# Attention and two feed-forward layers on one core: the softmax row sums of two head pairs in one PSUM bank, in 12 passes where there were 16

## The chip, the cores and the metric

The kernel runs on one core of a Trainium2 chip. The metric is device time in microseconds (us): the median over several executions. One more execution is recorded by the hardware profiler; the rows below come from it. PE is TensorE's matmul side, PEld its weight loads, DVE is VectorE, ACT ScalarE, POOL GpSimd, and SP issues DMAs.

## The reference

Batch 2, 12 heads, 448 positions, head width 64. Softcapped attention, then a gated layer behind an RMS norm, then a second layer with a leaky activation:

```python
scores = cap * np.tanh(scale * np.matmul(q, k.transpose(0, 1, 3, 2)) / cap)
attn = np.exp(scores - np.max(scores, axis=-1, keepdims=True))
attn = attn / (np.sum(attn, axis=-1, keepdims=True) + 1e-09)
x = np.matmul(attn, v)                     # then heads are put side by side: 896 x 768
rms = np.sqrt(np.mean(x * x, axis=-1, keepdims=True) + 1e-06)
xn = x / rms * rms_g
g = xn @ w_gate
x = (g * sigmoid(g) * (xn @ w_val)) @ w_out
h = x @ w_in
out = (np.maximum(h, 0) + alpha * np.minimum(h, 0)) @ w_out2
```

All of it is in fp32. This study is about the sum over a row of `attn` and what is done with its reciprocal.

## The kernel before, in words

The 24 heads are worked on as 12 **pairs**, numbered 0 to 11; two pairs that follow each other (0 and 1, 2 and 3, ...) form a **group**, numbered 0 to 5, and the program keeps them in `group` and `members`. One pass of the loop over `i` computes the scores of pair `i` and finishes pair `i - 1`. The order of the work is written out by hand: each engine has one queue of instructions that it takes in order, and a step that waits holds up everything behind it on its engine.

In iteration `i` TensorE does, in this order: for even `i` from 4 on, two *spread* matmuls of the pairs `i - 4` and `i - 3` (in `norm`, on `sel_t` and `r2`, before and after the first piece of scores); the scores of pair `i` in four pieces (`qk`); the row sums of pair `i - 1` (`sums`); the product of the weights with v of pair `i - 1` (`pv`, into `oo`). ScalarE takes the scores through tanh and exp (`soft`) into `pt`, seven tiles of 128 x 448 a pair: three keys' blocks of each of the two heads, and a seventh with the last 64 keys of both heads.

The row sums become a factor on the output on a way through several engines:

1. `sums(i)` sums over the 128 keys of a tile with a matmul whose weights are ones, 32 columns wide, so that four such matmuls run side by side in four column groups. Eight of them (the seventh tile counts twice, with half of the ones zeroed, `half`) fill four strips of 32 equal rows in the bank `us[i]`, two strips a head.
2. `evac_u(i)` copies the bank to `us` in SBUF (DVE) and issues two DMAs that lay the 448 sums of a row on 16 partitions (`gt`).
3. `recip(n)`, in the odd iteration after the group's second pair, adds the two strips and epsilon (`gf`), takes the reciprocal, splits it into a rounded part `th` and a rest `tl` (all DVE, 64 x 28 elements), and issues two DMAs that put both into `r2`.
4. The spread matmuls read `r2` in the next even iteration, and DVE multiplies the kept output `ee` by what they give (`xf`).

DVE also copies `oo` to `ee` (`evac_o`), splits q and k of the next pair into two parts `hi` and `lo` (`prep`), and unpacks the weights for the layers behind the attention (`w_bits`, into `wt`; `w_top`, `w_hi`, `w_lo`). POOL squares `xf` for the RMS norm (`square`) and adds weight tiles (`w_sum`, in `wt`). Which of these small steps stand in which iteration is set by two tables, `first` (filled by `a`) and `second` (filled by `z`), ahead of the loop. `xf`, `wt`, `th` and the other names are those of the rows below.

Of the kernel before, what the change touches and what calls it, by code (L numbers as in the profile page):

```python
# [35 lines left out]
Q = 32  # L36
K3 = KD // 2
# [20 lines left out]
def attn_moe_kernel(ctx: ExitStack, tc: tile.TileContext, units, qk_in, v, sel, w, gvec, alpha, out):  # L58
# [22 lines left out]
    half = aconst.tile([P, 2, D], F32, name="half")  # L81
# [116 lines left out]
    def third():  # L198
        return ps_x.tile([P, 2, 512], F32, tag="x", name="s")
# [41 lines left out]
    def tiles_of(i):  # L241
        return [pt[i][:, min(n, TILES - 1)] for n in range(TILES + 1)]
# [23 lines left out]
    def evac_u(i, queues=(nc.sync, nc.sync)):  # L266

        n, j = group[i]
        if j == 0:
            gt[n] = sb.tile([4 * RP, 2, S // RP], F32, tag="gt", name="gt")  # L270
        u = sb.tile([P, S], F32, tag="us", name="us")
        nc.vector.tensor_copy(u, us.pop(i)[:, :S])
        r0 = 2 * RP * j
        for k, q in enumerate(queues):
            q.dma_start(
                out=gt[n][r0:r0 + 2 * RP, k, :], in_=u[k * Q:P:D].rearrange("h (p s) -> h p s", p=RP)
            )

    def recip(n, queues=(nc.sync, nc.sync)):
        t = gt.pop(n)  # L280
        w = 2 * len(members[n])
        m = slice(0, w * RP)
        f = sb.tile([4 * RP, S // RP], F32, tag="gf", name="gf")
        nc.vector.scalar_tensor_tensor(
            out=f[m], in0=t[m, 0], scalar=eps_t[m], in1=t[m, 1], op0=ALU.add, op1=ALU.add
        )
        nc.vector.reciprocal(out=f[m], in_=f[m])
        th = sb.tile([4 * RP, S // RP], F32R, tag="th", name="th")
        tl = sb.tile([4 * RP, S // RP], F32R, tag="tl", name="tl")
        nc.vector.tensor_copy(th[m], f[m])  # L290
        nc.vector.tensor_tensor(out=tl[m], in0=f[m], in1=th[m], op=ALU.subtract)
        rr = r2[n % 2]
        for r0, x, q in zip((0, 32), (th, tl), queues):
            row = rr[r0:r0 + w].rearrange("r (p s) -> r p s", p=RP)
            q.dma_start(out=row.bitcast(F32), in_=x[m].bitcast(F32))
# [20 lines left out]
    def under():  # L316
        return ps_r.tile([P, 512], F32, tag="u", name="rps")

    def norm(i, rps):
        b, p = divmod(i, NP)  # L320
        n, j = group[i]
        nc.tensor.matmul(rps[:, :S], sel_t[:, j, :], r2[n % 2], start=True, stop=True)
        nc.vector.tensor_tensor(out=xf[b][:, p, :], in0=ee.pop(i), in1=rps[:, :S], op=ALU.mult)

# [89 lines left out]
    with tc.manual_schedule():  # L414
# [6 lines left out]
        nc.vector.memset(half, 0.0)  # L421
        for h in range(2):
            nc.vector.memset(half[h * D:h * D + D, h], 1.0)
# [37 lines left out]
        def a(i, fn, *args):  # L461
            first.setdefault(i, []).append((fn, args))
# [13 lines left out]
        for i in range(NPAIR):  # L476
            a(i, load_raw, i + 2)
# [29 lines left out]
        for i in range(NPAIR):  # L507
# [35 lines left out]
            if i:  # L543
                evac_u(i - 1)
                if i > 1:
                    pv(i - 1)
                del pt[i - 1], hi[i - 1], lo[i - 1], vt[i - 1]
# [4 lines left out]
        norm(last - 3, third()[:, 0])  # L552
        norm(last - 2, under())
# [3 lines left out]
        evac_u(last, (nc.sync, nc.scalar))  # L557
# [3 lines left out]
        def pair_tile(pool, tag):  # L561
            return pool.tile([P, 2, 512], F32, tag=tag, name=tag)

# [17 lines left out]
        product(pb[1], ("g", 1, "A12"), "B21", True, rows=(0,), span=range(6))  # L581
# [7 lines left out]
        product(pb[1], ("g", 1, "A12"), "B21", True, rows=(0,), span=range(6, 3 * K3))  # L589
# [13 lines left out]
        n_chain = [0]  # L603

        def chain_pair():
            n_chain[0] += 1
            return pair_tile(*((ps_x, "x") if n_chain[0] % 2 else (pm, "m")))

# [58 lines left out]
        for g in range(2):  # L667
            keep_part(d11, g, pb, lambda: h_of(g)[:, 2:])
            pa[g] = chain_pair()
            product(pa[g], ("g", g, "A11"), "B11", True, cuts={} if g else {(0, 4): SHORT})  # L670
# [675 lines left out]
```

## Time and profile before

| | |
|---|---|
| median of 3 runs | 552.42 us (552.24 to 552.92) |
| the profiled execution, time | 552.85 us |
| the profiled execution, span from first to last instruction | 551.1 us |
| mean granted clock of TensorE, as a share of full speed | 0.999 |
| busy: PE, PEld | 545.6 us (99%), 461.3 us (84%) |
| busy: DVE, ACT, POOL | 448.5 us (81%), 370.6 us (67%), 98.8 us (18%) |
| attention, up to the first product of the layers | 100.6 us of the span |

A row of the timeline reads: start in us from the start of the span, length in us, engine (a q behind it means its sequencer, which issues), line, operation, what is written<-what is read, shape, and how many alike are merged; in brackets the idle time of the engine just before it and what ended that. Instructions of one engine overlap by up to a tenth of a microsecond at their ends, and matmuls more. An fp32 matmul is two PE instructions, so eight matmuls are 16 instructions in a row's count.

### The profile page before, as it was taken

What the parts mean: (1) busy time and instruction counts of PE and PEld (TensorE: products, weight loads), DVE (VectorE), ACT (ScalarE), POOL (GpSimd) and SP (SyncE); (2) the same over time, 40 slices, a digit from 0 to 9 for tenths busy, and PEclk for the clock granted to TensorE, in tenths of its full rate; (3) what the DMA queues carried; (4) which work ended last, traced back from release to release, by engine and by line L of the source; (5) the groups of instructions that cost most, each with busy time, mean ns of one, the idle gap of its engine ahead of it and who ended that gap; (6) DMA issues with size and microseconds to landing.
All of it is one profiled execution on the core that took longest, in us unless ns stands there. A gap on an engine that the chain in (4) does not pass through costs nothing.

```text
span 551.1 us, 7691 instructions
## 1 busy us (share of the span) xinstructions
PE 545.6 (99%) x3061; PEld 461.3 (84%) x3061; DVE 448.5 (81%) x511; ACT 370.6 (67%) x433; POOL 98.8 (18%) x54
## 2 busy tenths in 40 slices
PE   8999999999999999999999999999999999999997
PEld 5444544699999999999999999999999999999996
DVE  4698889898999967878889898979866899999242
ACT  7989999477766554576757554787967996467110
POOL 0034663300065231010000048101111000000000
PEclk9999999999999999999999999999999999999999
DMA  7756420400334534065510573005512267013022
GB/s 253 260 188 197 164 73 8 163 12 1 120 120 162 178 110 171 1 228 173 184 46 1 229 230 114 1 0 173 172 58 69 105 203 255 0 59 115 0 101 100
DMA packets 17316, 66.09 MB, mean 120 GB/s; under 512 B 3584, under 2 KB 5504, under 8 KB 17280
## 3 DMA queue, kind: packets, MB, share of 16 engines
q1 hardware_dynamic: 16746, 65.08, 34.9%
q8 instruction: 24, 0.39, 0.3%
q10 hardware_dynamic: 390, 0.39, 0.2%
q0 software_dynamic: 144, 0.13, 0.1%
q14 instruction: 12, 0.10, 0.1%
HBM read 62.66 MB, written 2.75 MB: 119 GB/s over the span
## 4 chain that ended last, share of the span: by engine, by line
PE 96%; DVE 1%; ACT 1%; DMA 1%; issue 0%; DVEq 0%
PE s L395 19%; PE x L395 13%; PE m L395 13%; PE s L775 9%; PE s L749 8%; PE x L775 7%; PE oo L236 6%; PE s L207 5%; PE x L749 4%; PE m L775 4%; PE rps L249 3%; PE m L749 2%; PE s L408 1%; PE m L408 1%; PE x L408 1%; ACT pt L221 1%
## 5 line engine op out<-in xcount | busy, mean ns | idle before, releaser
L133 ACT CAST wh<-wt 128x768 fp32r<-128x768 f32 x105 | 87.1, 832 | 66.4 <-PE s L775 24.9
L139 DVE TENSOR_TENSOR wl<-wt,wh 128x768 fp32r<-128x768 f32 x108 | 113.6, 1053 | 12.5 <-ACT wh L133 12.2
L126 POOL TENSOR_TENSOR wt<-wt 128x768 f32<-128x768 f32 x33 | 75.1, 2284 | 265.9 <-DVE wt L118 97.9
L113 ACT CAST top<-raw 128x768 f16<-128x768 bf16 x64 | 68.8, 1076 | 27.0 <-DMA raw<-w_in 11.7
L118 DVE SCALAR_TENSOR_TENSOR wt<-raw,top 128x768 uint32<-128x768 uint32 x68 | 69.8, 1028 | 1.5 <-ACT top L113 1.5
L395 PE MATMUL s<-xx,wh 128*128 128x448 f32 x264 | 63.5, 364 | 0.0
L395 PEld LDWEIGHTS s<-xx,wh 128*128 128x128 f32 x264 | 49.4, 187 | 4.6 <-issue 0.7
L395 PE MATMUL x<-xx,wh 128*128 128x448 f32 x204 | 49.9, 366 | 0.0
L395 PE MATMUL m<-xx,wh 128*128 128x448 f32 x204 | 49.5, 364 | 0.0
L619 DVE TENSOR_TENSOR xx<-b,xx 128x896 fp32r<-128x896 f32 (+1 forms) x40 | 48.8, 1228 | 0.6 <-ACT xx L632 0.6
L216 ACT ACTIVATE pt<-s,cinv 128x896 f32<-128x896 f32 (+1 forms) x48 | 41.1, 911 | 6.2 <-PE s L207 5.9
L395 PEld LDWEIGHTS x<-xx,wh 128*128 128x128 f32 x204 | 38.2, 188 | 3.5 <-issue 0.4
L395 PEld LDWEIGHTS m<-xx,wh 128*128 128x128 f32 x204 | 38.2, 187 | 3.0
L775 PE MATMUL s<-xx,wh 128*128 128x448 f32 x132 | 40.0, 362 | 0.0
L236 PE MATMUL oo<-pt,vt 128*32 128x448 f32 x384 | 38.5, 540 | 0.4 <-ACT pt L221 0.3
L221 ACT ACTIVATE pt<-pt,cap_t 128x3136 f32<-128x3136 f32 (+2 forms) x13 | 35.3, 2714 | 0.4
L395 PE MATMUL s<-xx,wl 128*128 128x448 f32 x132 | 33.8, 364 | 0.0
L236 PEld LDWEIGHTS oo<-pt,vt 128*32 128x32 f32 x384 | 12.2, 110 | 23.6 <-issue 21.4
L775 PE MATMUL x<-xx,wh 128*128 128x448 f32 x104 | 31.2, 362 | 0.0
L749 PE MATMUL s<-xx,wh 128*128 128x448 f32 x96 | 27.2, 364 | 0.0
L775 PEld LDWEIGHTS s<-xx,wh 128*128 128x128 f32 x132 | 24.7, 187 | 2.1
L775 PE MATMUL s<-xx,wl 128*128 128x448 f32 x72 | 26.5, 367 | 0.0
(223 smaller groups left out, 1119.0 us busy)
## 6 DMA issues: line engine op xcount, KB each, us to landing
raw<-w_in SPq DMA_DIRECT2D x68, 768.0 KB
rw<-qk_in SPq DMA_DIRECT2D x11, 480.0 KB
vt<-v_in SPq DMA_DIRECT2D x12, 256.0 KB
out<-b SPq DMA_DIRECT2D x2, 448.0 KB
out<-b SPq DMA_DIRECT2D x2, 224.0 KB
out<-e SPq DMA_DIRECT2D x1, 448.0 KB
out<-c SPq DMA_DIRECT2D x2, 224.0 KB
gt<-us SPq DMA_DIRECT2D x23, 3.5 KB
```

Of the source, the lines that this page charges most:

```text
L113: copy(top_of[u].bitcast(F16)[:, 1::2], raw_t[u].bitcast(BF16)[:, 4:4 * n + 4:4])
L118: nc.vector.scalar_tensor_tensor(out=f_t[u].bitcast(U32), in0=raw_t.pop(u).bitcast(U32)[:, 1:2 * n + 1:2], scalar=13, in1=top_of.pop(u), o ...
L126: add(out=t, in0=f_t[a], in1=f_t[b], op=op)
L133: copy(h_t[u], f_t[u].rearrange("p (k m) -> p k m", m=P))
L139: nc.vector.tensor_tensor(out=l_t[u], in0=f_t[u].rearrange("p (k m) -> p k m", m=P), in1=h_t[u], op=ALU.subtract)
L216: nc.scalar.activation(out=t[:, 2 * g:2 * g + w], in_=st.pop((i, g))[:, :w, :S], func=AF.Tanh, scale=cinv)
L221: nc.scalar.activation(out=t[:, done:to], in_=t[:, done:to], func=AF.Exp, scale=cap_t)
L236: nc.tensor.matmul(oo[i][q * Q:q * Q + Q, :S], vv[:, n, q % 2 * Q:q % 2 * Q + Q], t[:, min(n, TILES - 1), :], start=c == 0, stop=c == TG, ...
L395: nc.tensor.matmul(ps[:, r, c0:c1], lhs, rhs[:, c0:c1], start=first and n == 0, stop=n == len(mm) - 1, skip_group_check=True,)
L619: nc.vector.tensor_tensor(out=out, in0=a, in1=b, op=op)
L749: nc.tensor.matmul(dst[m], wt[:, kk * MB + m, :], x, start=first and u == 0 and kk == 0 and n == 0, stop=u == 1 and kk == 1 and n == 2, sk ...
L775: nc.tensor.matmul(dst[m], wt[:, kk * MB + m, :], x, start=start and ks + kk == 0 and i == 0, stop=fin and last and kk == 1 and i == 2, sk ...
```

## The change

- A group's two pairs share one PSUM bank (`row_sum[n]`). Its four strips of 32 rows now hold four different rows each, picked by where ones stand in the weights: `strip` is a 56-column strip of zeros with 8 columns of ones, and a window of 32 columns of it puts a tile's sums on one of four groups of 8 rows. The seventh tile of a pair goes through once, with its own strip of half ones.
- For the group's first pair DVE adds the first two tiles to the next two (`add_halves`, 128 x 896, into `tp`), and TensorE sums the result in place of the four. With this the first pair has 4 matmuls in its own turn, and the second pair's turn has 8: one that is left of the first pair and its own seven. That makes 12 a group; before it was 8 and 8.
- `evac_u` runs once a group, with one copy and four DMAs of 64 partitions in place of two copies and two DMAs each. `recip` starts with one more DVE add, over 64 x 56 elements.
- The first spread matmul of a group writes to the second bank of the score tile that follows it, in place of the row-sum bank, and its multiplication by `ee` (`scaled`) stands behind it.
- Two casts and splits of weights for the layers (`w_hi`, `w_lo` of the first two of `conv`) stand one iteration later.
- Behind the loop, three matmuls of the layers stand ahead of the last two spreads that stood behind them, and three more ahead of the RMS sum.

The core of the diff:

```diff
+    def add_halves(i):
+        t = half_sum[i] = sb.tile([P, 2, S], F32, tag="tp", name="tp", bufs=1)
+        nc.vector.tensor_tensor(out=t, in0=pt[i][:, 0:2], in1=pt[i][:, 2:4], op=ALU.add)
 
     def sums(i):
-        us[i] = ps_s.tile([P, 2, 512], F32, tag="s", name="us")[:, 0] if i == NPAIR - 1 else under()
-        for n, t in enumerate(tiles_of(i)):
-            q = n % 2 * D + n // 2 % 2 * Q
+        n, j = group[i]
+        t, at_ = pt[i], lambda h: (0, 3 * UNIT - (2 * j + h) * UNIT)
+        tail = (t[:, TILES - 1], (1, 3 * UNIT - 2 * j * UNIT))
+        whole = [(t[:, c], at_(c % 2)) for c in range(TILES - 1)]
+        if j == 0:
+            row_sum[n] = under()
+            x = half_sum[i]
+            half_sum[i] = [(x[:, h], at_(h)) for h in range(2)]
+            steps = [*whole[4:], tail, half_sum[i][0]]
+        else:
+            steps = [half_sum.pop(i - 1)[1], *whole, tail]
+        for q, (x, (k, c)) in enumerate(steps):
+            q0 = q % 4 * Q
             nc.tensor.matmul(
-                us[i][q:q + Q, :S], half[:, n % 2, :Q] if n > 5 else ones[:, :Q], t, start=n < 4, stop=n > 3,
+                row_sum[n][q0:q0 + Q, :S], strip[:, k, c:c + Q], x, start=j == 0, stop=j == 1 and q > 3,
                 skip_group_check=True,
             )
...
+    def evac_u(n, queues=4 * (nc.sync,)):
+        gt[n] = sb.tile([4 * RP, 4, S // RP], F32, tag="gt", name="gt", bufs=1)
+        u = sb.tile([P, S], F32, tag="us", name="us", bufs=1)
+        nc.vector.tensor_copy(u, row_sum.pop(n)[:, :S])
+        for k in range(4):
+            queues[k].dma_start(
+                out=gt[n][:, k, :], in_=u[k * Q:k * Q + Q:UNIT].rearrange("r (p s) -> r p s", p=RP)
+            )
...
     def recip(n, queues=(nc.sync, nc.sync)):
         t = gt.pop(n)
+        nc.vector.tensor_tensor(out=t[:, 0:2], in0=t[:, 0:2], in1=t[:, 2:4], op=ALU.add)
...
         for i in range(NPAIR):
+            if i % 2 == 0:
+                (a if i else z)(i and i + 1, add_halves, i)
             a(i, load_raw, i + 2)
...
-        for n, j in ((3, 0), (4, 1), (9, 6)):
+        for n, j in ((4, 0), (5, 1), (9, 6)):
             z(n, w_hi, conv[j], nc.vector.tensor_copy)
...
-            if pairs:
-                norm(i - 4, under())
             if i:
                 home = {1: (ps_r, "u"), 2: (ps_o, "o")}.get(i)
-                qk(i, TG, home[0].tile([P, 1, 512], F32, tag=home[1], name="s") if home else third())
+                t = home[0].tile([P, 1, 512], F32, tag=home[1], name="s") if home else third()
+                if pairs:
+                    spread(i - 4, t[:, 1])
+                qk(i, TG, t)
+                if pairs:
+                    scaled(i - 4, t[:, 1])
...
-        product(pb[1], ("g", 1, "A12"), "B21", True, rows=(0,), span=range(6))
+        product(pb[1], ("g", 1, "A12"), "B21", True, rows=(0,))
         norm(last - 1, under())
...
+        pa[0] = chain_pair()
+        product(pa[0], ("g", 0, "A11"), "B11", True, rows=(0,), span=range(3))
         rms_sum(B - 1, upper("ms"))
```

What the change does to the queues is seen in two places. The first is DVE's queue in an odd iteration of the loop (iteration 7), from the copy of pair 5's output on; before it reads:

```order
L264 COPY ee<-oo 128x448
L190 CAST hi<-rw 128x960
L191 TENSOR_TENSOR lo<-rw,hi 128x960
L284 SCALAR_TENSOR_TENSOR gf<-gt,eps_t 64x28
L287 RECIPROCAL gf<-gf 64x28
L290 CAST th<-gf 64x28
L291 TENSOR_TENSOR tl<-gf,th 64x28
L118 SCALAR_TENSOR_TENSOR wt<-raw,top_95 128x768
L272 COPY us<-rps 128x448
```

After the change the same place of DVE's queue reads:

```order
L278 COPY ee<-oo 128x448
L246 TENSOR_TENSOR tp<-pt 128x896
L191 CAST hi<-rw 128x960
L192 TENSOR_TENSOR lo<-rw,hi 128x960
L292 TENSOR_TENSOR gt<-gt 64x56
L296 SCALAR_TENSOR_TENSOR gf<-gt,eps_t 64x28
L299 RECIPROCAL gf<-gf 64x28
L300 CAST th<-gf 64x28
L301 TENSOR_TENSOR tl<-gf,th 64x28
L119 SCALAR_TENSOR_TENSOR wt<-raw,top_95 128x768
```

The two new adds, `tp` and `gt`, stand ahead of the reciprocal, and the copy `us` of an even pair, which stood behind it, is gone.

The second place is TensorE's queue where iteration 7 ends and iteration 8 begins (the row sums of pair 6, the product with v, the first spread of group 2, and the first scores of pair 8); before it reads:

```order
L249 MATMUL rps<-pt,ones 32x448 x6
L249 MATMUL rps<-pt,half 32x448 x2
L236 MATMUL oo<-pt,vt 32x448 x16
L322 MATMUL rps<-r_0_92,sel_t 128x448
L207 MATMUL s<-hi 128x448
```

After the change it reads:

```order
L263 MATMUL rps<-pt,strip 32x448 x3
L263 MATMUL rps<-tp,strip 32x448
L237 MATMUL oo<-pt,vt 32x448 x16
L330 MATMUL s<-r_0_92,sel_t 128x448
L208 MATMUL s<-hi 128x448
```

Four of the eight matmuls are gone, the last that is left reads DVE's sum `tp`, and the spread that reads `r2` stands ahead of the scores as it did.

## Rows read from the trace of the kernel before

**Rows 1.** The page, busy time in us, share of the span, instructions.

```profile
PE 545.6 (99%) x3061; PEld 461.3 (84%) x3061; DVE 448.5 (81%) x511; ACT 370.6 (67%) x433; POOL 98.8 (18%) x54
```

**Rows 2.** Timeline of PE: pair 7's row sums, then its product with v.

```profile
66.09 1.32 PE L249 MATMUL rps<-pt,ones 128*32 128x448 f32 x10
...
67.62 3.19 PE L236 MATMUL oo<-pt,vt 128*32 128x448 f32 x32
```

**Rows 3.** Timeline of PE: the first spread matmul of groups 0 to 3.

```profile
32.11 0.47 PE L322 MATMUL rps<-r,sel_t 128*128 128x448 f32 x1
...
47.48 0.47 PE L322 MATMUL rps<-r,sel_t 128*128 128x448 f32 x1
...
62.86 0.47 PE L322 MATMUL rps<-r,sel_t 128*128 128x448 f32 x1
...
79.51 0.47 PE L322 MATMUL rps<-r,sel_t 128*128 128x448 f32 x1 [0.19 <-DVE us L272]
```

**Rows 4.** Timeline of SP: the DMAs of `tl`, and of `gt`.

```profile
29.42 0.57 SPq L295 DMA_DIRECT2D r<-tl  x1
...
39.13 1.09 SPq L275 DMA_DIRECT2D gt<-us  x2
...
60.48 0.58 SPq L295 DMA_DIRECT2D r<-tl  x1
```

**Rows 5.** Timelines of ACT and PE: the exps of pairs 1 and 2, pair 1's sums.

```profile
16.66 2.92 ACT L221 ACTIVATE pt<-pt,cap_t 128x3136 f32<-128x3136 f32 x1
...
22.82 2.91 ACT L221 ACTIVATE pt<-pt,cap_t 128x3136 f32<-128x3136 f32 x1
...
19.99 1.32 PE L249 MATMUL rps<-pt,ones 128*32 128x448 f32 x10
```

**Rows 6.** Timeline of DVE, iteration 3, around the reciprocal of group 0.

```profile
25.31 0.65 DVE L190 CAST hi<-rw 128x960 fp32r<-128x960 f32 x1
26.00 1.16 DVE L191 TENSOR_TENSOR lo<-rw,hi 128x960 fp32r<-128x960 f32 x1
27.87 0.24 DVE L284 SCALAR_TENSOR_TENSOR gf<-gt,eps_t 64x28 f32<-64x28 f32 x1 [0.72 <-DMA gt<-us]
...
28.50 0.17 DVE L290 CAST th<-gf 64x28 fp32r<-64x28 f32 x1
```

**Rows 7.** Timeline of DVE, a sum of 128 x 896 from two SBUF tiles.

```profile
131.19 1.08 DVE L619 TENSOR_TENSOR b<-p,b 128x896 f32<-128x896 f32 x1
```

**Rows 8.** Timeline of DVE, iteration 5, around the reciprocal of group 1.

```profile
41.00 0.62 DVE L264 COPY ee<-oo 128x448 f32<-128x448 f32 x1
...
43.29 0.23 DVE L284 SCALAR_TENSOR_TENSOR gf<-gt,eps_t 64x28 f32<-64x28 f32 x1
```

**Rows 9.** Timelines of POOL and DVE, iteration 7.

```profile
54.97 1.84 POOL L126 TENSOR_TENSOR wt<-wt 128x768 f32<-128x768 f32 x1
...
55.51 0.62 DVE L264 COPY ee<-oo 128x448 f32<-128x448 f32 x1 [0.98 <-PE oo L236]
56.05 1.27 DVE L190 CAST hi<-rw 128x960 fp32r<-128x960 f32 x1
...
58.96 0.24 DVE L284 SCALAR_TENSOR_TENSOR gf<-gt,eps_t 64x28 f32<-64x28 f32 x1 [0.44 <-DMA gt<-us]
```

**Rows 10.** Timelines of POOL and DVE, iteration 9.

```profile
70.62 5.43 POOL L126 TENSOR_TENSOR wt<-wt 128x768 f32<-128x768 f32 x3
...
72.68 0.62 DVE L521 COPY spare<-ms 128x448 f32<-128x448 f32 x1 [1.17 <-PE ms L339]
...
74.68 1.40 DVE L290 CAST th<-gf 64x28 fp32r<-64x28 f32 x1
```

**Rows 11.** Timelines of DVE and PE, copies of pairs 8 and 9, pair 10's product.

```profile
79.84 0.62 DVE L264 COPY ee<-oo 128x448 f32<-128x448 f32 x1
...
89.46 0.56 DVE L264 COPY ee<-oo 128x448 f32<-128x448 f32 x1
...
92.28 3.19 PE L236 MATMUL oo<-pt,vt 128*32 128x448 f32 x32
```

More of the change, by code (lines that the diff above doesn't have):

```diff
@@ L36 @@
 Q = 32
+UNIT = Q // 4
 K3 = KD // 2
@@ L80, in attn_moe_kernel @@
     ones = aconst.tile([P, P], F32, name="ones")
-    half = aconst.tile([P, 2, D], F32, name="half")
+    strip = aconst.tile([P, 2, 7 * UNIT], F32, name="strip")
     sel_t = aconst.tile([P, 2, P], F32R, name="sel_t")
@@ L280, in recip @@
         t = gt.pop(n)
-        w = 2 * len(members[n])
-        m = slice(0, w * RP)
-        f = sb.tile([4 * RP, S // RP], F32, tag="gf", name="gf")
+        nc.vector.tensor_tensor(out=t[:, 0:2], in0=t[:, 0:2], in1=t[:, 2:4], op=ALU.add)
+        f, th, tl = (
+            sb.tile([4 * RP, S // RP], dt, tag=x, name=x, bufs=1) for x, dt in (("gf", F32), ("th", F32R), ("tl", F32R))
+        )
         nc.vector.scalar_tensor_tensor(
-            out=f[m], in0=t[m, 0], scalar=eps_t[m], in1=t[m, 1], op0=ALU.add, op1=ALU.add
+            out=f, in0=t[:, 0], scalar=eps_t[:4 * RP], in1=t[:, 1], op0=ALU.add, op1=ALU.add
         )
[L287 to L292, printed above, removed]
+        nc.vector.reciprocal(out=f, in_=f)
+        nc.vector.tensor_copy(th, f)
+        nc.vector.tensor_tensor(out=tl, in0=f, in1=th, op=ALU.subtract)
         for r0, x, q in zip((0, 32), (th, tl), queues):
-            row = rr[r0:r0 + w].rearrange("r (p s) -> r p s", p=RP)
-            q.dma_start(out=row.bitcast(F32), in_=x[m].bitcast(F32))
+            row = r2[n % 2][r0:r0 + 4].rearrange("r (p s) -> r p s", p=RP)
+            q.dma_start(out=row.bitcast(F32), in_=x.bitcast(F32))
     def square(i):
@@ L317, in under, with spread, scaled, norm @@
         return ps_r.tile([P, 512], F32, tag="u", name="rps")
-    def norm(i, rps):
-        b, p = divmod(i, NP)
+    def spread(i, rps):
         n, j = group[i]
         nc.tensor.matmul(rps[:, :S], sel_t[:, j, :], r2[n % 2], start=True, stop=True)
+    def scaled(i, rps):
+        b, p = divmod(i, NP)
         nc.vector.tensor_tensor(out=xf[b][:, p, :], in0=ee.pop(i), in1=rps[:, :S], op=ALU.mult)
+    def norm(i, rps):
+        spread(i, rps)
+        scaled(i, rps)
     def join_squares(b):
@@ L420, in attn_moe_kernel @@
         nc.vector.memset(rms_b, RMS_EPS)
-        nc.vector.memset(half, 0.0)
+        nc.vector.memset(strip, 0.0)
+        nc.vector.memset(strip[:, 0, 3 * UNIT:4 * UNIT], 1.0)
         for h in range(2):
-            nc.vector.memset(half[h * D:h * D + D, h], 1.0)
+            nc.vector.memset(strip[h * D:h * D + D, 1, (3 + h) * UNIT:(4 + h) * UNIT], 1.0)
         for t in tops:
@@ L551, in attn_moe_kernel @@
         evac_o(last - 1)
-        norm(last - 3, third()[:, 0])
-        norm(last - 2, under())
+        both = third()
+        for fn in (spread, scaled):
+            for j in range(2):
+                fn(last - 3 + j, both[:, j])
         sums(last)
@@ L556, in attn_moe_kernel @@
             square(j)
-        evac_u(last, (nc.sync, nc.scalar))
+        evac_u(len(members) - 1, (nc.scalar, nc.sync, nc.sync, nc.sync))
         pv(last)
@@ L562, in pair_tile, with chain_pair @@
             return pool.tile([P, 2, 512], F32, tag=tag, name=tag)
+        n_chain = [0]
+        def chain_pair():
+            n_chain[0] += 1
+            return pair_tile(*((ps_x, "x") if n_chain[0] % 2 else (pm, "m")))
         def ct(name):
@@ L588, in attn_moe_kernel @@
         lows(late)
-        product(pb[1], ("g", 1, "A12"), "B21", True, rows=(0,), span=range(6, 3 * K3))
         sum4("g", 1)
         product(pb[1], ("g", 1, "A12"), "B21", True, rows=(1,))
+        pa[0] = chain_pair()
+        product(pa[0], ("g", 0, "A11"), "B11", True, rows=(0,), span=range(3))
         rms_sum(B - 1, upper("ms"))
@@ L668, in attn_moe_kernel @@
             keep_part(d11, g, pb, lambda: h_of(g)[:, 2:])
-            pa[g] = chain_pair()
-            product(pa[g], ("g", g, "A11"), "B11", True, cuts={} if g else {(0, 4): SHORT})
+            if g:
+                pa[1] = chain_pair()
+                product(pa[1], ("g", 1, "A11"), "B11", True)
+            else:
+                product(pa[0], ("g", 0, "A11"), "B11", True, rows=(0,), span=range(3, 3 * K3), cuts={(0, 4): SHORT})
+                product(pa[0], ("g", 0, "A11"), "B11", True, rows=(1,))
         w_hi(("g", 1, "S1"))
```

20 lines of the change are left out of this document (3 added, 17 removed).

## The prediction

> **What bounds the kernel now.** The page comes first: PE is busy for 545.6 us of a span of 551.1 [rows 1]. A kernel like this gets faster by each matmul that is taken away, but only as long as what the matmuls wait for comes earlier too. So the second view is the timeline of PE at the places where it reads something that another engine must have finished, and the third is that something. The place that matters is the first spread matmul of each group [rows 3]: it reads `r2`, which comes out of row sums, a copy, two hops of DMA and four small DVE steps. PE does not wait there for the DMA (the only bracket, 0.19 us in the last row, names the copy `us`). How near it is to waiting shows when each spread is set against the DMA that feeds it: the DMA of `tl` is issued at 29.42 and 60.48 [rows 4], the spreads start at 32.11 and 62.86, so the landing took at most 2.69 and 2.38 us. From the start of `gf` to the spread there are 4.24 us in group 0 (27.87 to 32.11), 4.19 in group 1 (43.29 to 47.48) and 3.90 in group 2 (58.96 to 62.86) [rows 3, 6, 8, 9].
>
> **What is saved.** Pair 7's eight sum matmuls last from 66.09 to 67.62 [rows 2], four at a time, so a round of four is 0.76 us. Each group loses one round, all of them in the turn of its first pair (8 to 4; the second pair keeps 8). Six rounds are 4.6 us. The first can't be kept whole: pair 1's sums start at 19.99 and need its exp, which ends at 16.66 + 2.92 = 19.58 [rows 5] and is set by ScalarE, so 0.41 remains of 0.76. PE alone would gain 0.41 + 5 x 0.76 = 4.2 us.
>
> **What the way of `r2` costs.** I call the time from the start of `gf` to the first possible spread the tail. `gf`, the reciprocal and `th` take 0.80 (27.87 to 28.50 + 0.17) [rows 6]; the DMA of `tl` is issued 0.75 after that (28.67 to 29.42) [rows 4, 6]; then it has to land. No row gives the landing alone. It is over 0.57, the issue itself, and at most 2.38; I take 2.0, near the upper end, since that bound is from the same transfer in the same queue and the lower is only its issue. The tail is then 3.6 us, with bounds of 2.1 and 3.9.
>
> The new add `tp` has the shape and the kind of operands of a row that takes 1.08 us [rows 7], some 1.0 until the next one starts. It stands ahead of the reciprocal on DVE. The new add over `gt` is bounded below by nothing and above by `gf`, 0.24 with its turnaround [rows 6]; I take 0.24, as a step that the next one reads. The four DMAs of `gt` take 1.1 us more to issue than two (two take 1.09 [rows 4]); DVE is busy with `hi` and `lo` meanwhile, so I put them at nothing; if DVE came earlier, the 0.72 and 0.44 us in which it waits for `gt` now [rows 6, 9] would grow by up to 1.1. The copies `us` that go stand behind the reciprocal and don't help it. The moved casts stand behind it too; they leave iteration 3 and enter iteration 5, and in both no spread reads anything behind them, so nothing; if the next copy of a product had to wait for them, their time would fall on PE.
>
> Group by group, in the clock of the kernel before:
>
> - Group 0. `tp` needs pair 2's exp, which ends at 22.82 + 2.91 = 25.73 [rows 5]. Then 1.0 for it, 0.69 for `hi`, 1.1 for `lo` [rows 6], 0.24 for `gt`: `gf` at 28.8 in place of 27.87, spread at 28.8 + 3.6 = 32.4. PE would be there at 32.11 - 0.41 - 0.76 = 30.9. It waits 1.5 and is 0.3 later than now [rows 3].
> - Group 1. `ee` at 41.3, and from it to `gf` 2.29 now [rows 8] and 1.0 + 0.24 more: `gf` at 44.8, spread at 48.4, now 47.48. It is 0.95 late.
> - Group 2. `ee` at 55.51 + 0.95, so `tp` is asked for at 57.0. POOL's weight sum lies there, 54.97 + 0.95 to 57.76 [rows 9]. What happens to DVE then is in the same rows: `hi`, 0.65 alone [rows 6], takes 1.27 there, until POOL's op is done. So `tp` runs from 57.76 to 58.76, `gf` starts at 60.8, the spread at 64.4, now 62.86: 1.5 late. Without that hold it would be 0.8.
> - Group 3. The copy `spare` moves from 72.68 to 74.2, `tp` is asked for at 74.75. POOL's three sums fill 70.62 + 1.5 to 77.6, 1.81 each [rows 10]; `th`, 0.17 alone, took 1.40 against them. `tp` gets in between the second and the third (75.8 to 76.8), the third ends at 78.6, `gt`'s add behind it; `gf` at 78.8, spread at 82.4, now 79.51: 2.9 late.
> - Iterations 10 and 11. `th` ends at 79.6 in place of 74.68 + 1.40 = 76.08 [rows 10]. From there to `ee` of pair 8 is 3.76 now [rows 11], 0.54 less without a copy: 82.8. Then 9.62 to `ee` of pair 9, 0.54 and 1.0 for `tp`: 94.0. The last matmul of pair 10's round reads it, 0.76 for its two halves, so that the product starts at 94.8, now 92.28 [rows 11]. 2.5 us late, with that group's round already counted.
>
> From there on PE has 450 us of matmuls with next to no waits, whose number the change leaves as it is; I see nothing that gives the 2.5 us back. The three matmuls (0.6 us) put ahead of the last spreads and of the RMS sum only move covers. The profiled execution took 552.85, 0.43 above the median of 552.42; I put the difference on the median: **554.9 us**.
>
> **The skill's rule on the port.** The rows show `hi` at 1.27 beside 0.65 and `th` at 1.40 beside 0.17, each under a POOL op. The Trainium skill's page "SBUF — State Buffer", section "Who interferes with whom", says that VectorE and GpSimd share a port pair as an exclusive lock, that a VectorE instruction with two SBUF inputs contends with a GpSimd one that reads SBUF, and that the later one blocks fully. By that rule `tp` waits as I have it. Were it free of it, as adds are that read PSUM, groups 2 and 3 would be the 0.8 and -0.3 of the rival below.
>
> **Rivals.**
>
> - *PE sets the time.* All of 4.2 us is gained: 548.2. For it: PE is the busy engine, and no spread waits for a DMA today. Against: it takes a tail under 2.2 us in group 0 (30.9 - 28.8), so a landing of about 0.6 us, the lower bound. Chance 0.14.
> - *The adds miss POOL's ops.* Groups 0 and 1 as above, group 2 0.8 late; in iteration 9 `gf` starts at 72.68 + 0.54 + 0.8 + 1.24 = 75.3, the tail ends at 78.9, before PE, which gets there 0.3 earlier than now, and some 0.3 more remain of pair 10's round: 0.5 us gained, 551.9. It decides by whether POOL's queue ends before 74 us. POOL is full from 64 us on, and its first weight sum waits for a DVE step that comes later. Chance 0.16.
> - *Later still.* The tail is 3.9 instead of 3.6, and the four loops carry 0.3 each: 556.1. Chance 0.08, beyond the forecast's own 0.62.
>
> **Numbers.** The likeliest is 554.9, its own range 553.5 to 556.4. I can tell from no change what differs by over 0.2%, 1.1 us. The middle rival is inside that. Faster 0.14, same 0.16, slower 0.70. The range for 8 in 10 takes in the middle rival and the upper bound of the tail: 551.0 to 556.4; the first rival stays out.
>
> **What would show it.** In the changed kernel's trace, PE's sums of an even pair should last half as long as now, 0.76 us. The first spread of groups 0 to 3 should carry idle time of 1 to 2.5 us behind a DMA on `r2`. `tp` should last 1.1 us in iterations 1, 3 and 5 and near 1.8 or more in 7 and 9. PE's first product behind the attention, now at 100.6, should start near 103. If the spreads don't wait, or `tp` is never held, the sum is wrong at that term, and the time falls to the rivals'.

## The result, and the profile after

The changed kernel takes **557.29 us** (median of 4 executions, 556.85 to 558.03), the kernel before 552.43 in the same runs: a ratio of 1.0088, 95% interval 1.0070 to 1.0105. It is 4.86 us slower. The prediction was 554.9 with a range of 551.0 to 556.4, so the direction was right and the time lies 0.9 us above the range. The execution that the trace shows took 558.03, 5.18 more than the one of before.

First the page of the changed kernel: span, busy times, and the shares of the chain that ended last.

```profile
span 556.2 us, 7589 instructions
...
PE 544.3 (98%) x3013; PEld 462.9 (83%) x3013; DVE 454.4 (82%) x518; ACT 370.3 (67%) x433; POOL 99.6 (18%) x54
...
PE 86%; DVE 5%; DMA 3%; ACT 2%; issue 1%; SPq 1%; DVEq 0%
```

48 matmul instructions are gone and PE is busy 1.3 us less [rows 1], yet the span is 5.1 us longer: the time went into waits, and in one stretch into a lower clock (below). PE's share of the chain is down from 96% to 86%; DVE, DMA and SP hold a part of it. What PE's matmuls waited for between 20 and 106 us is one row of the view of waits (total us, times, longest):

```profile
PE s L330 <- DMA r<-tl: 6.0, 4, 2.0
```

The same stretch of before has one wait of 0.2 us. The four are the first spreads of groups 0 to 3, with pair 10's product and the first product of the layers behind them, in the timeline of PE:

```profile
32.43 0.44 PE L330 MATMUL s<-r,sel_t 128*128 128x448 f32 x1 [1.06 <-DMA r<-tl]
...
49.32 0.44 PE L330 MATMUL s<-r,sel_t 128*128 128x448 f32 x1 [1.99 <-DMA r<-tl]
...
65.53 0.44 PE L330 MATMUL s<-r,sel_t 128*128 128x448 f32 x1 [1.49 <-DMA r<-tl]
...
83.65 0.44 PE L330 MATMUL s<-r,sel_t 128*128 128x448 f32 x1 [1.49 <-DMA r<-tl]
...
97.25 3.19 PE L237 MATMUL oo<-pt,vt 128*32 128x448 f32 x32
...
105.82 0.87 PE L410 MATMUL s<-xx,wh 128*128 128x448 f32 x3
```

Against [rows 3, 11] and the forecast, in us from the start of the span:

| | before | forecast | after | later than forecast |
|---|---|---|---|---|
| spread of group 0 | 32.11 | 32.4 | 32.43 | 0.0 |
| spread of group 1 | 47.48 | 48.4 | 49.32 | 0.9 |
| spread of group 2 | 62.86 | 64.4 | 65.53 | 1.1 |
| spread of group 3 | 79.51 | 82.4 | 83.65 | 1.25 |
| product of pair 10 | 92.28 | 94.8 | 97.25 | 2.45 |
| first product of the layers | 100.64 | near 103 | 105.82 | |

From the last row on nothing moves: 105.82 - 100.64 = 5.18 is the whole difference of the two profiled executions. So all of it lies in the attention, and the error of 2.4 us has three places: 0.9 in group 1, 0.35 in groups 2 and 3, 1.2 between group 3 and pair 10.

**Group 1.** Timelines of DVE (iterations 4, 5 and 9) and POOL:

```profile
33.51 0.62 DVE L334 TENSOR_TENSOR xf<-ee,s 128x448 f32<-128x448 f32 x1 [1.46 <-PE s L208]
...
34.58 1.08 DVE L191 CAST hi<-rw 128x960 fp32r<-128x960 f32 x1
...
41.72 0.62 DVE L278 COPY ee<-oo 128x448 f32<-128x448 f32 x1
42.25 1.08 DVE L246 TENSOR_TENSOR tp<-pt 128x896 f32<-128x896 f32 x1
...
43.93 1.16 DVE L192 TENSOR_TENSOR lo<-rw,hi 128x960 fp32r<-128x960 f32 x1
45.36 0.21 DVE L292 TENSOR_TENSOR gt<-gt 64x56 f32<-64x56 f32 x1 [0.27 <-issue]
45.61 0.24 DVE L296 SCALAR_TENSOR_TENSOR gf<-gt,eps_t 64x28 f32<-64x28 f32 x1
...
75.89 2.26 DVE L246 TENSOR_TENSOR tp<-pt 128x896 f32<-128x896 f32 x1
78.08 1.83 DVE L292 TENSOR_TENSOR gt<-gt 64x56 f32<-64x56 f32 x1
79.95 0.24 DVE L296 SCALAR_TENSOR_TENSOR gf<-gt,eps_t 64x28 f32<-64x28 f32 x1
...
73.57 6.28 POOL L127 TENSOR_TENSOR wt<-wt 128x768 f32<-128x768 f32 x3
```

`tp` takes the forecast's 1.08 us here. `ee` starts at 41.72 instead of 41.3, and from it to `gf` are 3.89 us instead of 2.29 + 1.24 = 3.53. The chain that ended last shows why in the second stretch (start, length, what):

```profile
41.75 3.08 DMA gt<-us
...
44.86 0.05 DVEq L292
44.91 0.45 issue
45.36 0.22 DVE gt L292
...
47.13 2.06 DMA r<-tl
49.19 0.14 issue
49.32 0.44 PE s L330
```

The last of the four DMAs of `gt` is issued at 41.75 and lands at 44.83; DVE's add starts half a microsecond after that, 0.36 later than if it had followed `lo` as in group 0. DVE's four small steps are not what holds here, the DMA is. The 0.36 is that of this execution: in the profiled executions of E4, E9 and E10, the same program up to iteration 7, the add starts 0, 0 and 0.38 us later than `lo` alone would let it in group 1, and 0.33, 0.53 and 0 in group 2. So each has 0.3 to 0.5 us of this hold on the way, in one group or the other. The second hop, `tl`, takes 2.06 us as I had it (2.0).

**Group 3 to pair 10.** `tp` is held to 2.26 us and the small add over `gt` to 1.83 by POOL's three sums, as forecast. What was not forecast is the next view, the granted clock behind the wait (us, PE busy and count, clock, DMA share, GB/s):

```profile
core 0: us, PE busy (x), PEclk, DMA share, GB/s
...
82.20:83.70 1.50, 0.05 (x1) 1.00 0.36 87
...
85.40:89.00 3.60, 3.60 (x24) 0.53 0.00 0
```

A microsecond and a half in which PE does next to nothing is followed by 3.6 us at, in the mean, 0.53 of full speed, so nearly all of it at the lower of the two levels, 1.2 GHz. The scores and sums that stand there (85.06 to 89.69, 4.63 us) took 3.06 before.

### The profile page after: what moved, and what is told of

It reads as the page before. It is cut to its first block, busy times and chain, and to the rows that moved or that the text cites. A ratio compares the mean times of both kernels' runs of the same rounds, so it can differ in the third digit from the quotient of the medians.

```text
span 556.2 us, 7589 instructions
## 1 busy us (share of the span) xinstructions
PE 544.3 (98%) x3013; PEld 462.9 (83%) x3013; DVE 454.4 (82%) x518; ACT 370.3 (67%) x433; POOL 99.6 (18%) x54
## 4 chain that ended last, share of the span: by engine, by line
PE 86%; DVE 5%; DMA 3%; ACT 2%; issue 1%; SPq 1%; DVEq 0%
PE s L410 18%; PE x L410 12%; PE m L410 12%; PE s L804 9%; PE s L778 8%; PE x L804 7%; PE x L778 4%; PE m L804 3%; PE m L778 2%; PE s L208 2%; PE oo L237 2%; DMA r<-tl 1%; DMA gt<-us 1%; PE s L423 1%; ACT pt L217 1%
## 5 line engine op out<-in xcount | busy, mean ns | idle before, releaser
L237 PE MATMUL oo<-pt,vt 128*32 128x448 f32 x384 | 39.7, 540 | 0.4 <-ACT pt L222 0.4
L410 PE MATMUL s<-xx,wl 128*128 128x448 f32 x132 | 33.8, 364 | 0.0
L237 PEld LDWEIGHTS oo<-pt,vt 128*32 128x32 f32 x384 | 13.9, 110 | 22.0 <-issue 18.3
L410 PE MATMUL x<-xx,wl 128*128 128x448 f32 (+1 forms) x104 | 26.6, 365 | 0.0
```

The lines of the kernel that those rows point to most:

```text
L237: nc.tensor.matmul(oo[i][q * Q:q * Q + Q, :S], vv[:, n, q % 2 * Q:q % 2 * Q + Q], t[:, min(n, TILES - 1), :], start=c == 0, stop=c == TG, ...
L410: nc.tensor.matmul(ps[:, r, c0:c1], lhs, rhs[:, c0:c1], start=first and n == 0, stop=n == len(mm) - 1, skip_group_check=True,)
```

## The experiments

Two theories. **The way of `r2`** (mine): DVE's steps ahead of the reciprocal, POOL's hold on them, and two DMA hops set when a spread can start; what PE saves is then only waited away. **The shared bank itself** (the rival): it costs what it saves, wherever the steps stand (four DMAs, the moved multiplication, a fuller DVE).

All ratios are against the kernel before, run on the same chip.

**E1. The shared bank without the adds.**

```diff
-            if i % 2 == 0:
-                (a if i else z)(i and i + 1, add_halves, i)
...
-            steps = [*whole[4:], tail, half_sum[i][0]]
-        else:
-            steps = [half_sum.pop(i - 1)[1], *whole, tail]
+        steps = [*whole, tail]
```

> The changed kernel without VectorE's adds `tp`: TensorE sums all 14 tiles of a group, seven in each pair's turn; the shared bank, the four DMAs of `gt`, the add over `gt` and the place of `scaled` stay. Changed kernel 557.3 us, kernel before 552.4. Theory of the chain (the DVE steps ahead of `r2` set the time): the way to `r2` is 1.0 us shorter a group and TensorE gets to the spreads 0.75 us a group later, so nearly all waits go: 553.0 to 554.3 us. Rival (the adds are hidden; the shared bank with its four DMAs and the moved multiplication cost the time): 557 us or more, since TensorE has its six rounds back.

554.35 us, ratio 1.0036 (1.0023 to 1.0049), 0.05 above the range of the theory of the way. PE's waits for `r2`:

```profile
PE s L326 <- DMA r<-tl: 2.3, 3, 1.1
```

The adds, with the waits and the lower clock that follow from them, are 2.9 of the 4.9 us lost, although without them TensorE has its rounds back. But 2.0 us are lost without them: three waits of 0.5 to 1.1 us are left. That part belongs to the rest of the change, so the rival holds a piece of the truth. Whether it is the extra add over `gt`, the four DMAs, the moved multiplication or the moved casts, E1 doesn't tell apart.

**E2. The reciprocal earlier.** `recip` ahead of `hi` and `lo`, and the load of `raw` behind the DMAs of `gt`:

```diff
-                steps.insert(i < 9, (recip, (i - 3) // 2))
+                steps.insert(0, (recip, (i - 3) // 2))
...
-                    a(i, w_next, conv[i - 2])
+                    (a if i % 2 else z)(i, w_next, conv[i - 2])
```

> The changed kernel with two moves: the steps from the add over `gt` to `tl` stand ahead of `hi` and `lo` in iterations 3, 5 and 7 (as they already do in 9), and the load of `raw` is issued behind the DMAs of `gt` instead of ahead of them. No arithmetic changes. Theory of the chain: the waits of groups 0, 1 and 2 (1.06, 1.99 and 1.49 us) shrink to 0, about 0.2 and about 0.4; that of group 3 and the half clock behind it stay: 553.3 us, range 552.8 to 554.5. Rival (the DMA's landing alone sets it, whatever the order on VectorE): group 0 keeps its wait, 555.5 us or more.

558.56, ratio 1.0112 (1.0095 to 1.0129): slower still. The theory missed; the rival's bound (555.5 us or more, the landing sets it) held. The chain of this kernel in group 1, and SP's timeline:

```profile
41.16 1.71 DMA gt<-us
...
44.76 4.66 DMA r<-tl
49.42 0.14 issue
49.55 0.44 PE s L330
```

```profile
41.74 0.46 SPq L103 DMA_DIRECT2D raw<-w_in  x1
42.24 0.43 SPq L178 DMA_DIRECT2D rw<-qk_in  x1
42.77 0.38 SPq L183 DMA_DIRECT2D vt<-v_in  x1
...
44.76 0.59 SPq L304 DMA_DIRECT2D r<-tl  x1
```

`gt` now lands 1.71 us after its last issue in place of 3.08, and the reciprocal is 2.4 us earlier. But `raw`, `rw` and `vt` (768, 480 and 256 KB) now stand right ahead of `r2` in SP's queue, and `tl` takes 4.66 us to land in place of 2.06. The wait was moved from one hop to the other, and the 2.81 us that PE now waits in group 1 are followed by 3.4 us at a mean clock of 0.52 (51.0 to 54.4). The Trainium skill's page "DMA: Bandwidth & Descriptors", section "Queues, rings and completion order", says that each DMA engine takes descriptors in the order of the ring; the two rows agree. My step that priced a landing from the nearest row was blind to what is issued just ahead.

**E5, E11. The bulk behind both hops.** The load of `raw` of an even iteration goes behind the DMAs of `r2` of the next one (E5, which keeps E2's early reciprocal). E11 adds `hi` ahead of the multiplications in iterations 4 and 6.

```diff
-                    a(i, w_next, conv[i - 2])
+                    due.append(conv[i - 2])
+                while i % 2 and due:
+                    a(i, w_next, due.pop(0))
```

> The changed kernel with the steps from the add over `gt` to `tl` ahead of `hi` and `lo` in iterations 3, 5 and 7, as in the run before, but with the load of `raw` of an even iteration issued in the next one, behind the DMAs of `r2`, so that 768 KB fewer lie in SP's queue ahead of `gt` and of `r2`. In the run before, the last DMA of `r2` landed 4.7 us after its issue in group 1, against 2.1 in the changed kernel. Theory (the way of `r2` sets the time, and both its hops wait behind whatever bulk load was issued just ahead of them): it lands within 2 to 2.7 us in groups 0 to 2, those waits go to under 0.8 us each, group 3 keeps its 1.5 and the lower clock behind: 553.9 us, range 553.0 to 555.0. Rival (the earlier steps don't help because TensorE waits for something else too): 557 us or more.

> The changed kernel in another order: reciprocal steps ahead of `hi` and `lo`, loads of `raw` behind the DMAs of `r2`, and `hi` ahead of the multiplications that wait for the spreads in iterations 4 and 6 alone. Casts and GpSimd as changed. Theory: the waits of groups 0 to 2 go but for some 0.3 us; that of group 3 (GpSimd) and the lower clock stay: 554.8 us, range 554.0 to 555.9. Rival (without the earlier cast VectorE's loop is still too long): the same as the run with the later loads alone, 555.9.

E5: 555.94, ratio 1.0062 (1.0047 to 1.0077). E11: 553.81, ratio 1.0024 (1.0015 to 1.0034). In E5 the waits at the first spreads of groups 0 to 2 fall to none, 0.30 and 0.57 us; in E11 there is none at all. In group 1 of E5 `tl` is issued at 43.62 and the spread starts at 45.90, so it lands within 2.3 us with `rw` and `vt` still ahead of it: in E2 it was the 768 KB of `raw` that cost most. E5 missed its range by 0.9; the spread of group 3 now waited 2.65 us, and group 1's second spread 0.89 for `ee`. E11, where group 3 waits 2.71, came out 0.2 below its range. What the first groups give back, group 3 waits away, behind POOL's sums (E3, E14).

**E3, E10, E9. Group 3 and POOL.** E3 leaves out six of POOL's sums; E10 has two of them made by DVE behind `us` of iteration 8; E9 leaves out `tp` of pair 8.

```diff
+        if out in skip:
+            f_t[out] = f_t[a]
+            return
         t = f_t[home] if home else f_tile()
```

> The changed kernel leaves out six of GpSimd's weight sums (S1, S2 and S3 of the first layer's two groups; a neighbouring tile stands in for each, so the output isn't the reference's). Theory of the chain with the hold by GpSimd: `tp` takes 1.1 us in iteration 9 in place of 2.26 and the add over `gt` 0.2 in place of 1.83; the spread of group 3 doesn't wait any more (1.49 us) and the clock stays at its upper level (1.57 us): 554.2 us, range 553.5 to 554.8. In iteration 7 the landing of `gt` holds VectorE instead, so group 2 gains next to nothing. Rival (the long `tp` and `gt` adds have nothing to do with GpSimd): 557.3 us.

> The changed kernel, but two of GpSimd's three weight sums of iteration 8 (S2 of the second group, S3 of the first) are made by VectorE, behind the copy `us` of iteration 8, where it waits for TensorE anyway. Theory (GpSimd's queue of sums holds `tp` and the add over `gt` in iteration 9): the queue is two sums shorter there, the reciprocal of group 3 comes 1.5 us or more earlier, the wait of group 3 and the lower clock behind it go: 554.2 us, range 553.5 to 555.2. Rival (VectorE is full: what it does more it finishes later): 557 us or more.

> The changed kernel, but the pairs 8 and 9 have no add `tp`: TensorE sums their 14 tiles. It is the `tp` of pair 8 that stands ahead of the reciprocal of group 3 on VectorE (in iteration 9); the run that left out that of pair 6 left out the wrong one. Theory (in iteration 9 GpSimd's three sums hold `tp` and the steps behind it): without `tp` the add over `gt` and the reciprocal get through about one GpSimd sum earlier (0.75 us or more), TensorE comes 0.75 us later, the wait of group 3 falls from 1.5 us to near nothing and the clock stays up (1.57 us): 555.0 us, range 554.2 to 555.8. Rival (the wait hangs on the add over `gt` alone, which GpSimd holds all the same): 557 us.

E3: 554.59, ratio 1.0037 (1.0022 to 1.0052), as expected. Its DVE in iteration 9, against 2.26 and 1.83 in the changed kernel:

```profile
75.40 1.08 DVE L251 TENSOR_TENSOR tp<-pt 128x896 f32<-128x896 f32 x1
76.40 0.20 DVE L297 TENSOR_TENSOR gt<-gt 64x56 f32<-64x56 f32 x1
76.64 0.24 DVE L301 SCALAR_TENSOR_TENSOR gf<-gt,eps_t 64x28 f32<-64x28 f32 x1
```

So POOL is what holds them (in iteration 7 too: `tp` takes 1.08 in place of 2.08). The rule of the Trainium skill's page "SBUF — State Buffer", section "Who interferes with whom", that the prediction weighed holds in these rows. Group 3's wait is gone, the clock stayed up in the profiled execution. E10, 555.88 (1.0053 to 1.0079), also has no wait at that spread, but DVE, busier with two sums, brings `ee` of pair 7 later: PE waits 1.65 us for it ahead of the RMS sum, and the lower clock now lies behind that wait (0.53 from 76.0 to 79.6 us). E9, 556.04 (1.0048 to 1.0074), loses group 3's wait too, but there the wait of group 2 was 2.06, with the lower clock behind it (0.51 from 66.6 to 70.1), and the time gained little. E9 lies 0.2 above its range, E10 0.7.

**E4. The clock.** Seven small matmuls of ones fill the wait of group 3:

```diff
+                if i == 10:
+                    for _ in range(7):
+                        nc.tensor.matmul(t[:, 1, :P], ones, ones, start=True, stop=True)
                 if pairs:
                     spread(i - 4, t[:, 1])
```

> The changed kernel with seven 128x128 matmuls of ones ahead of the spread of group 3, into the bank half that the spread then overwrites; no result changes. Theory (the fall to the lower clock between 85.4 and 89 us is a result of TensorE's wait of 1.49 us at 82.2): with less of that stretch empty the clock stays at its upper level, iteration 10's scores and sums take 1.57 us less: 555.7 us. Rival (the clock falls there for another reason, or the stretch is still too empty): 557.3 us.

556.47, ratio 1.0079 (1.0063 to 1.0094). Timeline of PE, and the same window as above:

```profile
81.45 1.83 PE L534 MATMUL s<-ones 128*128 128x128 f32 x14
```

```profile
85.40:89.00 3.60, 3.60 (x36) 1.00 0.00 0
```

36 instructions in the place of 24, at full clock. From the spread of group 3 (83.03) to the first product (103.94) are 20.91 us, in the changed kernel 105.82 - 83.65 = 22.17: 1.26 us less for work that does nothing. The change's four executions all have a mean clock of 0.997; of E4's, three have 0.999 or 1.000 and one 0.995 all the same. The median fell by 0.8 only, against 1.6 expected, and the intervals of the two ratios overlap: it is the clock that shows the link here, not the time.

**E6, E7, E8. Two mistakes of mine.** E6 is E5 with one weight cast back in iteration 3 and `hi` early in all even iterations. E7 is E5 without `tp` of pair 6. E8 is all together.

```diff
-        for n, j in ((4, 0), (5, 1), (9, 6)):
+        for n, j in ((3, 0), (5, 1), (9, 6)):
...
-            if i % 2 == 0:
+            if i % 2 == 0 and i != 6:
                 (a if i else z)(i and i + 1, add_halves, i)
```

> As the run with the later loads, and two more moves on VectorE: the cast and split of the first of `conv` one iteration earlier, as before the change (the second stays), and the cast `hi` of an even iteration ahead of the multiplications that wait for the spreads. Theory (what VectorE does between a spread and the next reciprocal is a loop that is longer than TensorE's own work of two iterations): 2.5 us of it leave that loop, what is left of the waits of groups 1 and 2 goes: 553.3 us, range 552.3 to 554.2. Rival (VectorE's order doesn't matter any more once the loads are out of the way): the same as that run.

> As the run with the later loads, but group 3 (pairs 6 and 7) has no add `tp`; TensorE sums its 14 tiles. Theory (in group 3 GpSimd holds `tp` and what follows, 1.2 us): TensorE has 0.75 us more to do there, the wait falls from 1.5 to 0.5 or less and the clock stays at its upper level (1.57 us): 1.8 us less than that run, about 552.1, range 551.3 to 553.3. Rival (the wait of group 3 comes from the lateness of the earlier groups): no less than that run.

> All moves of the three runs sent with it together: reciprocal early, loads later, one cast earlier, `hi` early, no add in group 3. Theory: TensorE waits less than 0.5 us at each spread, five of the six rounds are saved: 550.5 us, range 549.0 to 552.2, faster than the kernel before (552.4). Rival (the shared bank costs as much as it saves wherever the steps stand): 552.5 us or more.

E6: 554.08 (1.0020 to 1.0046), as expected. E7, 554.96 (1.0032 to 1.0066), and E8, 554.49 (1.0026 to 1.0056), lie 1.7 and 2.3 above their ranges. The add that stands ahead of group 3's reciprocal is that of pair 8, not of pair 6: I had taken out one that held nothing there. In E8 group 3 still waits 1.5 us, a second spread 0.9 for an `ee` that the early cast delays, and 1.2 go to scores that wait for ScalarE, behind a multiplication that an early `hi`, held by POOL to 1.98 us, delays.

**E12. Order and sums together** (E11 and E10).

> The last two together: the other order, and two of GpSimd's sums on VectorE. Theory (TensorE's saving of six rounds shows once `r2` is never late): no wait over 0.5 us at a spread, the clock up throughout: 551.2 us, range 550.0 to 552.6, faster than the kernel before. Rival (VectorE, 0.7 us a group and two sums fuller, is the bound now): 553.5 us or more.

553.70, ratio 1.0022 (1.0010 to 1.0034), 1.1 above its range. The longest wait of PE between 20 and 106 us:

```profile
PE ms L358 <- DVE ee L282: 2.7, 1, 2.7
```

No spread waits any more; E10's new wait has taken their place. The twelve executions lie apart by their mean clock: three at 1.000 took 552.3 to 552.4, the others, at 0.993 to 0.997, 553.6 to 555.7.

**E13, E14. That wait taken away too.** The RMS sum of iteration 9 behind two score tiles, `us` of iteration 8 ahead of `wt`, and `tp`, reciprocal, `spare` in this order. Both keep E11's order otherwise. E14 leaves POOL's sums as the change has them; E13 makes S2 of the second group on DVE in iteration 8 and both S3 on DVE behind the loop.

```diff
             for g in range(TG - 1):
                 qk(i, g, two())
...
+            if i == 9:
+                add_halves(8)
+                recip(3)
+                rms_sum(0, upper("ms"))
+                rms_keep(0)
+                nc.vector.tensor_copy(rstd[0], ms_of[0][:, :S])
+                ms_of[0] = rstd[0]
...
+        z(8, lambda: sum2("g", 1, add=nc.vector.tensor_tensor))
...
+        for g in range(2):
+            sum3("g", g, add=nc.vector.tensor_tensor)
```

> The order of the last run, with the new wait that it met taken away: the RMS sum of iteration 9 stands behind two score tiles in TensorE's queue, so that `ee` of pair 7 and GpSimd's last square needn't be ready so early; `us` of iteration 8 ahead of `wt`; `tp`, the reciprocal of group 3 and only then the copy `spare`; S2 of the second group on VectorE in iteration 8, both S3 on VectorE behind the loop. Theory (the six rounds are really saved, and each late operand ahead of a TensorE step hides them): the 2.70 us go, the spreads wait under 0.5 us, first product of the layers near 98 us: 550.2 us, range 549.3 to 551.8, faster than the kernel before (552.5). Rival (VectorE is too full with `tp`): 552.5 us or more.

> The same with GpSimd's sums where the changed kernel has them. Theory (GpSimd's sums hold `tp` and the reciprocal of group 3): `tp` or the add over `gt` takes 1.8 us or more in iteration 9, the spread of group 3 waits 1 us or more: 552.0 us, range 551.0 to 553.5. Rival (with these steps earlier GpSimd's sums lie behind them): the same as the run sent with it.

E13 takes **549.72 us** (549.68 to 550.02), ratio 0.9956 (0.9942 to 0.9969), as expected: faster than both kernels and, by the two ratios, 7.3 us faster than the change as it stood. PE in it, from 20 us to the first product of the layers:

```profile
20.00:97.00 77.00, 77.00 (x685) 34.88 (x677) 70.37 (x101) 70.72 (x60) 30.40 (x20) 1.00 0.39 130
```

The same stretch of the kernel before, from 20 to 100 us:

```profile
20.00:100.00 80.00, 79.78 (x727) 36.88 (x729) 69.05 (x96) 71.70 (x61) 35.37 (x23) 1.00 0.41 131
```

The spread of group 3 and the first product of the layers in E13:

```profile
76.59 0.47 PE L334 MATMUL s<-r,sel_t 128*128 128x448 f32 x1
...
97.53 0.87 PE L414 MATMUL s<-xx,wh 128*128 128x448 f32 x3
```

PE is busy for 77.00 of 77.00 us (the second and third numbers of the row), at full clock, and the layers start at 97.53 in place of 100.64: 3.1 of the 4.2 us that the rounds are worth (2.4 between the medians). That it is the rounds and not the new order alone, before's row shows: there PE stood idle for 0.22 us in 80, so another order had next to nothing to give in that stretch. E14 takes 555.17 (1.0037 to 1.0066), 1.7 above its range and 5.4 above E13. DVE and POOL in its iteration 9, and PE:

```profile
69.22 1.82 DVE L250 TENSOR_TENSOR tp<-pt 128x896 f32<-128x896 f32 x1
70.96 1.83 DVE L296 TENSOR_TENSOR gt<-gt 64x56 f32<-64x56 f32 x1
72.83 1.72 DVE L300 SCALAR_TENSOR_TENSOR gf<-gt,eps_t 64x28 f32<-64x28 f32 x1
...
74.93 1.37 DVE L304 CAST th<-gf 64x28 fp32r<-64x28 f32 x1
...
70.05 6.22 POOL L127 TENSOR_TENSOR wt<-wt 128x768 f32<-128x768 f32 x3
...
77.10 6.01 PE L241 MATMUL oo<-pt,vt 128*32 128x448 f32 x32 [3.63 <-DVE spare L564]
```

Three POOL sums hold three small steps of DVE one after the other (`gt`, `gf` and `th`: 56 or 28 elements a partition, 1.4 to 1.8 us each), up to the end of POOL's queue at 76.27. Only then does `spare` free the bank for pair 8's product. So PE's wait, expected at the spread, stands at this product, 3.63 us, and the product takes 6.01 us in place of 3.19 (the mean clock is 0.80 from 70 to 80 us and 0.86 from 80 to 90).

**E15. The moved multiplication back behind its spread.**

```diff
-                qk(i, TG, t)
                 if pairs:
                     scaled(i - 4, t[:, 1])
+                qk(i, TG, t)
```

> The changed kernel with the multiplication `scaled` back right behind its spread, ahead of the three score matmuls that write the other bank of the same tile. Theory (in the changed kernel the multiplication starts 0.3 us later behind its spread because it waits for those three): VectorE's loop is 0.3 us shorter between groups 0 and 1, the scores wait for the multiplication instead, about 0.7 us at each of four spreads: 557 to 559 us. Rival (the banks are told apart and nothing waits): 556.7 us.

557.87, ratio 1.0109 (1.0090 to 1.0128), as expected. Timelines of DVE and PE:

```profile
32.36 0.62 DVE L334 TENSOR_TENSOR xf<-ee,s 128x448 f32<-128x448 f32 x1 [0.85 <-PE s L330]
...
33.03 0.48 PE L208 MATMUL s<-hi 128*128 128x448 f32 x1 [0.71 <-DVE xf L334]
```

The multiplication now starts as its spread ends; in exchange scores that wait for it cost PE 3.2 us in four places. That the change has the better end of this wait is not shown by the time: the intervals of the two ratios overlap.

## Why the prediction was wrong in size

**What held, step by step.** The mechanism: all four spreads waited for the DMA on `r2`, 1.06 to 1.99 us, where 1 to 2.5 were forecast. The rounds: an even pair's sums last 0.77 us (27.40 to 28.17). The tail from `gf` to the spread, forecast 3.6: 3.64, 3.71, 3.63 and 3.70 in the four groups. Group 0 to 0.03 us. Group 2's and group 3's hold by POOL: `tp` lasts 2.08 and 2.26 (E3 shows the cause by taking POOL's sums away). The rival in which PE sets the time, 548.2, was right only about what the rounds are worth once the way is clear: E13 comes to 1.5 us of it. The first round was not kept, 0.07 us in place of 0.41: PE waited 0.40 at 17.28 for pair 2's `lo`, which comes no earlier than before. Group 0's wait swallowed that. The rival *later still*, 556.1, was the nearest by number, but its tail of 3.9 is not what came. In the middle rival PE would reach group 3's spread some 0.15 us earlier than before, not 0.3 (62.86 + 0.8 + 16.46 - 0.76 = 79.36), which moves its time by 0.2 and nothing else.

Three terms of the sum failed: the DMAs of `gt`, put at nothing (0.36 us in this execution); the multiplication behind the spread, left out (some 0.3); and, the largest, the price of group 3's wait, taken as its length alone (1.2 more).

**What failed: "The four DMAs of `gt` take 1.1 us more to issue than two ... so I put them at nothing".** DVE's `hi` and `lo` were to cover them. In group 1 they didn't: the last landing, at 44.83, let the add start at 45.36, and `lo` alone would have let it start at 45.00, so 0.36 us. The prediction named what it would cost without cover, but didn't set the landing against the new place of the add. Behind E2 and E5 stands the larger form of the same error: with a bulk load ahead of it, either hop takes 1.4 to 2.6 us longer.

**What was left out: the spread's product.** In group 1 `ee` starts 0.4 us later than forecast. From the spread to the first `hi` behind it are 2.15 us (32.43 to 34.58), before 1.86 (32.11 to 33.97), since `scaled` now waits for three scores as well. That is 0.3 of the 0.4; the rest is `hi`, 1.08 in place of 0.96. It is read from these rows; E15 shows that the wait is real, but moves it, so the 0.3 by itself stays argued. Together with 0.1 from the tail, these are group 1's 0.9 us, and groups 2 and 3 inherit them; 0.2 more in group 2 is POOL's sum, which also starts later (57.18), and 0.1 in group 3 the tail.

**What failed most: the step from group 3's spread to "the product starts at 94.8".** It took iteration 10's work at the length that it had before, with no term for what a wait does to the work behind it, and let DVE set that product (`ee` of pair 9, then `tp`). From the spread at 83.65 on, the chain that ended last runs on PE alone, and 1.57 us of it are the lower clock. At full clock PE's way from the spread to the product would be 12.0 us (before 79.51 to 92.28, less a round of 0.76), the forecast's by DVE is 12.4, the measured one 13.6: so of the 1.57 some 1.2 show. Without them the time would have been near 556.1 (an estimate from these rows), inside the range. E4 and the stretches behind the waits of E2, E9 and E10 show the link; when it happens stays open.

0.9 + 0.35 + 1.2 = 2.45, the whole gap between the forecast's 94.8 and 97.25.

**What stays open.** No run tells how E1's 2.0 us divide among the add over `gt`, the four DMAs, the moved multiplication and the moved casts. `gt` in fewer DMAs, or over another queue, wasn't tried. Nor is it settled why the clock falls behind some waits and not behind others (below), and with it the scatter of E12.

## What to carry to other kernels

When a change takes work from the busiest engine, follow the longest loop that feeds it through the other engines and queues, and set each landing against the new place of its reader: here 3.9 us of matmuls were saved in the profiled execution, and 6.0 us of waits at the spreads, 1.6 of lower clock and as much in small losses came in their place (the largest of these, 0.9, at pair 8's row sums, which wait for the held `tp`). In these runs a small transfer landed later by 1.4 to 2.6 us when a bulk load was issued just ahead of it, so moving a step earlier can be worth nothing (E2) until the bulk is moved too (E5, E11). And the saving was real: it showed when every late operand on that loop had been moved, the steps that GpSimd held among them, and not before.

## What the runs showed of the hardware that I had not expected

- A wait can cost twice. Behind 1.49 us of idle PE came 3.6 us at a mean clock of 0.53. But in the same execution the waits of groups 1 and 2, 1.99 and 1.49 us, were followed by none. The same length of wait in E6 and E8 (1.48 and 1.49 us at the same spread) was followed by none in the profiled executions (mean clock 1.000), nor was E11's of 2.71; E10's of 1.65 and E9's of 2.06 were. E12's twelve executions of one program show both. The Trainium skill's page "TensorE: Matmul & The Clock Gate", section "Part 1: The HAM clock gate", says that the clock follows how busy the engine has been. The rows agree in that each fall found here stands behind a wait, of 1.49 us or more; they don't tell which wait it will be.
- A chain of small DVE steps can pay for a POOL operation at each step: in E14 `gt`, `gf` and `th` took 1.83, 1.72 and 1.37 us against 0.20, 0.24 and 0.17 alone. `th` is a cast with one operand, held as in [rows 10]. The Trainium skill's page "SBUF — State Buffer", section "Who interferes with whom", says that copies and casts can enter a mode that uses the shared pair; the row agrees.
- The view of waits can name a releaser that only ends at about the same time. In E5 and E11 it puts the 2.65 and 2.71 us of group 3 down to ScalarE's `spare`. But by the trace's semaphore events the DMA of `tl` landed at 81.15 and 80.05 there, 0.14 us ahead of the spreads (81.29, 80.19), the distance of every other spread that waited (49.19 to 49.32 in the chain above), and the spread reads `r2`, not `spare`. In E2 the wait of group 0, put down to ScalarE's exp, is the same: `tl` landed at 31.71, the spread started at 31.84.
